# Attention and two expert layers on one core: expert sums in three half-token banks, five banks for attention, and a new order

## The chip, the cores and the metric

The kernel runs on one core of a Trainium2 chip. The metric is the device time of one execution in microseconds (us); lower is better. The core has a matrix engine (PE, TensorE), a vector engine (DVE, VectorE), an activation engine (ACT, ScalarE), a general engine (POOL, GpSimd) and a queue engine for transfers (SP, SyncE). PE adds up its results in eight banks (PSUM) of 512 fp32 columns for each of 128 partitions; DVE and ACT read them there.

## The reference, cut to what matters

```
q_p, k_p = phi(q * 64**-0.25), phi(k * 64**-0.25)      # phi: exp(x @ omega.T - max over the 128 features)
kv, z = sum_s k_p v, sum_s k_p
x = (q_p kv) / (q_p z)                  # 4 batches x 8 heads x 576 tokens x 64 -> 2304 x 512
for layer in (moe, moe2):               # 8 experts, 512 -> 1024 -> 512, one expert for each token
    e = argmax(x @ w_gate);  y = gate * relu(x @ w1[e]) @ w2[e]     # moe: also a sigmoid gate
    x = y
```

The inputs are such that nearly all tokens of a batch choose the same expert. The kernel computes that expert for the whole batch of 576 tokens and mends the tokens that chose another one in a small block at the end.

## The kernel before, in words

Attention works on 16 pairs of heads, four for each batch of 576 tokens (`FORMS` and `TILED` give the form of each). A pair goes through the steps `load_q`, `load_kv`, `q_split`, `q_proj`, `q_exp`, `q_cut`, `k_proj`, `kv`, `num`, `den_a` to `den_c` and `norm`. `k_proj` asks for four PSUM banks at once (`features`, with two calls of `heads`), and all of its matmuls stand ahead of the reads that free these banks. `q_proj` comes in two kinds: where `TILED` is "1" for the batch, one call serves both heads with K = 64 matmuls in fp32 and takes four banks at once; otherwise `q_split` cuts q into a high and a low part first and each head has a call of its own with four fp32r matmuls into two banks. In form "S" `num` is three fp32r products with 288 columns for each half of the tokens, after `q_exp` has made a rounded copy (`qh`) and `q_cut` the rest (`ql`); in form "F" it is one fp32 product, and `q_cut` and the copy fall away.

There are eight expert units, one for each layer and batch, in the order of `ORDERS[3]`. In a unit, `up` makes eight groups (`fc`) of 24 matmuls of 288 columns each, and `down` makes four groups (`c`) of 48. Three matmuls stand for one exact product (high by high, high by low, low by high). A group is one tile `pm` of two banks, one for each half of the tokens, and the halves alternate in the innermost loop. After a group of `up`, ACT writes the relu (`hh`) and DVE the rest (`hl`), each 576 columns wide; after a group of `down`, DVE multiplies by the gate weights (`y`). There are two such tiles, four banks together (`psm`), and the other four (`psa`) serve attention, the gates and the small block. Only the last group of the last unit is done half by half.

The instruction stream is written by one program that gives PE the expert matmuls and calls `slot()` in between; a slot may start up to two attention steps, chosen by a key (`WEIGHTS`, `TWEAKS`) among those that an estimate of the engines' clocks (`Estimate`) calls ready. `Engine` calls go to their queue in the order of the program, and each engine works its queue in order. Before the first unit only attention runs, with seven banks of `psa`; `fill()` gives PE idle matmuls on zeros when nothing is ready. `gate` makes the routing of a batch in several stages, and one bank tile of it (`pg`, `pt`, `pc` or `ptc`) stays in use between two stages. `COPIES` and `START_COPIES` say which engine makes which copy: 0 ACT, 1 DVE, 2 ACT or DVE by an argument (nothing given: ACT).

Of the kernel before, what the change touches and what calls it, by code (L numbers as in the profile page):

```python
# [11 lines left out]
F32 = mybir.dt.float32  # L12
F32R = mybir.dt.float32r
# [11 lines left out]
HS = S // 2  # L25
# [16 lines left out]
TILED = "1100"  # L42
# [11 lines left out]
FORMS = "FRRRFFFSSSSSSSSS"  # L54
CW = 132
XW = 4

WEIGHTS = (-99.0, -99.0, 262.75, -267.46, 198.55, 332.25, -310.29, -471.44, -33.14, 239.82, -489.57, 351.55, -254.05, 173.97)
RAW_WEIGHTS = (-99.0, -99.0, -374.05, -379.93, 519.94, 42.51, 947.74, -153.49, 153.44, 733.35, -182.45, -952.4, -419.2, -198.78)
# [4 lines left out]
PACE = (0.097, 0.001, 1.054, 1.126, 886.024, 3.696, 0.265, 0.264, 1.069, 256.941, 0)  # L64

COPIES = (1, 1, 2, 1, 0, 0, 2)

START_PACE = (0.142, 0.015, 7.433)
START_COPIES = (1, 2, 0, 1, 0, 0, 0)
TWEAKS = {  # L70
    ("den_a", 1): 44.7, ("den_a", 2): 595.6, ("den_a", 3): -18.8, ("den_a", 4): 323.2, ("den_a", 5): 525.4,
    ("den_a", 6): 291.8, ("den_a", 7): -101.8, ("den_a", 8): -71.9, ("den_a", 9): 56.6, ("den_b", 0): 325.6,
    ("den_b", 1): 1.1, ("den_b", 4): 37.9, ("den_b", 5): -9.0, ("den_b", 6): 171.8, ("den_b", 7): 121.2,
    ("den_b", 8): -64.0, ("den_b", 9): -127.0, ("den_c", 0): 75.6, ("den_c", 1): -98.6, ("den_c", 2): 478.0,
    ("den_c", 4): 37.6, ("den_c", 5): -237.6, ("den_c", 6): -550.8, ("den_c", 9): 0.0, ("den_w", 0): 345.4,
    ("den_w", 1): 143.8, ("den_w", 2): 574.5, ("den_w", 3): -16.2, ("den_w", 4): -57.6, ("den_w", 5): -71.8,
    ("den_w", 6): 77.2, ("den_w", 7): 20.5, ("den_w", 8): 24.7, ("den_w", 9): 7.5, ("k_proj", 0): 107.5,
    ("k_proj", 1): -20.1, ("k_proj", 2): 135.6, ("k_proj", 3): -98.0, ("k_proj", 4): -29.4,
    ("k_proj", 5): -51.0, ("k_proj", 6): -49.7, ("k_proj", 8): 473.1, ("k_proj", 9): -623.2, ("kv", 0): -176.7,
    ("kv", 1): -125.4, ("kv", 3): 483.1, ("kv", 4): -62.8, ("kv", 7): -51.7, ("kv", 8): -203.5,  # L80
    ("kv", 9): 650.0, ("norm", 0): 643.8, ("norm", 1): 542.2, ("norm", 2): 77.4, ("norm", 3): -45.2,
    ("norm", 4): -186.2, ("norm", 5): -106.9, ("norm", 6): 227.5, ("norm", 7): 48.0, ("norm", 8): -0.4,
    ("norm", 9): -5.1, ("num", 0): 0.5, ("num", 1): -19.9, ("num", 10): 26.1, ("num", 14): 416.8,
    ("num", 16): 22.8, ("num", 17): 45.6, ("num", 18): 55.1, ("num", 2): -74.7, ("num", 3): 19.4,
    ("num", 4): -844.8, ("num", 6): 170.0, ("num", 7): -558.5, ("q_cut", 1): -198.8, ("q_cut", 11): -85.3,
    ("q_cut", 12): 60.3, ("q_cut", 13): -72.2, ("q_cut", 14): -1186.5, ("q_cut", 16): -207.1,
    ("q_cut", 17): 478.9, ("q_cut", 19): -174.8, ("q_cut", 2): 25.9, ("q_cut", 3): -306.2, ("q_cut", 4): -287.7,
    ("q_cut", 5): -24.0, ("q_cut", 6): -93.1, ("q_cut", 7): -533.3, ("q_cut", 9): -21.1, ("q_exp", 0): -237.5,
    ("q_exp", 1): 916.5, ("q_exp", 10): -245.4, ("q_exp", 11): -365.4, ("q_exp", 13): -179.8,
    ("q_exp", 14): 179.6, ("q_exp", 15): -1328.8, ("q_exp", 17): 117.8, ("q_exp", 18): 181.2,  # L90
    ("q_exp", 19): -23.4, ("q_exp", 2): 343.6, ("q_exp", 3): -348.5, ("q_exp", 5): -38.0, ("q_exp", 6): -20.7,
    ("q_exp", 7): 4.5, ("q_exp", 9): 820.0, ("q_proj", 0): -488.4, ("q_proj", 1): 984.4, ("q_proj", 10): -817.3,
    ("q_proj", 11): -497.2, ("q_proj", 12): 68.1, ("q_proj", 13): -219.8, ("q_proj", 14): -554.4,
    ("q_proj", 16): -308.5, ("q_proj", 19): 96.0, ("q_proj", 3): -28.6, ("q_proj", 4): -32.0,
    ("q_proj", 5): 11.6, ("q_proj", 6): -43.9, ("q_split", 11): -396.2, ("q_split", 14): -317.9,
    ("q_split", 15): 29.6, ("q_split", 17): -159.4, ("q_split", 18): 101.6, ("q_split", 19): -14.0,
    ("q_split", 5): 27.3, ("q_split", 6): -34.7, ("q_split", 7): -89.0, ("q_split", 9): -848.8,
# [3 lines left out]
class Estimate:  # L101
# [24 lines left out]
    def clock(self, begin):  # L126
        while begin >= (self.window + 1) * 3.413:
            if self.slow:
                self.slow = self.work < 0.77 * 3.413
            else:  # L130
                self.slow = self.work < 0.4 * 3.413
            self.window += 1
            self.work = 0.0
        return 2 if self.slow else 1

    def run(self, engine, op, out, ins):
# [8 lines left out]
        elif engine == "tensor":  # L145
# [11 lines left out]
            if rows != self.rows:  # L157
                begin += 0.1
                cost += 0.107
                self.rows = rows  # L160
            cost *= self.clock(begin)
            self.work += cost
# [85 lines left out]
def attention_moe_moe_kernel(ctx, tc, qT, qT2, kT, vp, omst, wg1, wg2, w1a, w2a, w1b, w2b, tabs, eye, outT):  # L248
# [587 lines left out]
    class Unit:  # L836
# [57 lines left out]
        def up(self, x, need, slot):  # L894
            self.h = []
            for fc in range(NFC):
                need(self, fc // 2)
                w = self.w[fc // 2]
                pm = pl.psm.tile([128, 2, 512], F32, tag="pm", name="pm")
                for c in range(NDC):  # L900
                    for i, (wi, xi) in enumerate(((0, 0), (0, 1), (1, 0))):
                        for s in range(2):
                            nc.tensor.matmul(
                                pm[:, s, :HS],
                                w[wi][:, c, fc % 2],
                                x[xi][:, c, tokens(s)],
                                start=c == 0 and i == 0,
                                stop=c == NDC - 1 and i == 2,
                            )
                    if c < NDC - 1:  # L910
                        slot()
                hh = pl.mp.tile([128, 2, HS], F32R, tag="hh", name="hh", bufs=8)
                hl = pl.mp.tile([128, 2, HS], F32R, tag="hl", name="hl", bufs=8)
# [5 lines left out]
                slot()  # L919

        def down(self, need, slot, put, halves=None):
            for c in range(NDC):
                need(self, 4 + c)
                w = self.w[4 + c]
                if halves is not None and c == NDC - 1:
                    pm = pl.psm.tile([128, 2, 512], F32, tag="pm", name="pm")
                    for s in range(2):
                        y = pl.mp.tile([128, S], F32, tag="y", name="y", bufs=4)
                        for fc in range(NFC):
                            for i, (wi, hi) in enumerate(((0, 0), (0, 1), (1, 0))):  # L930
                                nc.tensor.matmul(
                                    pm[:, s, :HS],
                                    w[wi][:, fc, :],
                                    self.h[fc][hi][:, s, :],
                                    start=fc == 0 and i == 0,
                                    stop=fc == NFC - 1 and i == 2,
                                )
                            if fc == 3 or fc == NFC - 1 and s == 0:
                                slot()
                        t = tokens(s)  # L940
                        nc.vector.tensor_tensor(out=y[:, t], in0=pm[:, s, :HS], in1=self.cb[:, t], op=ALU.mult)
                        halves(c, y, s)
                    return
                pm = pl.psm.tile([128, 2, 512], F32, tag="pm", name="pm")
                for fc in range(NFC):
                    for i, (wi, hi) in enumerate(((0, 0), (0, 1), (1, 0))):
                        for s in range(2):
                            nc.tensor.matmul(
                                pm[:, s, :HS],
# [5 lines left out]
                    if fc < NFC - 1:  # L955
                        slot()
                y = pl.mp.tile([128, S], F32, tag="y", name="y", bufs=4)
                nc.vector.tensor_tensor(
                    out=y.rearrange("p (s t) -> p s t", s=2),
                    in0=pm[:, :, :HS],  # L960
                    in1=self.cb.rearrange("p (s t) -> p s t", s=2),
                    op=ALU.mult,
                )
                put(c, y)
                slot()
# [252 lines left out]
    with tc.manual_schedule():  # L1218
# [128 lines left out]
        def run_unit(n, opens=None, block=None):  # L1347
# [11 lines left out]
            if n == 0:  # L1359
                pl.psi = None  # L1360
                psums.close()
                pl.psm = pool(ctx, "psm", 2, space=PSUM)
                pl.psa = pool(ctx, "psa", 4, space=PSUM)
# [15 lines left out]
            else:  # L1379
# [5 lines left out]
                def put(c, y):  # L1385
                    if block is not None:
                        nc.vector.scalar_tensor_tensor(
# [102 lines left out]
```

## Time and profile before

| | before |
|---|---|
| median of 3 runs | 588.97 us (588.17 to 589.77) |
| the profiled execution's own time | 588.86 us |
| its span, first to last instruction | 587.1 us |
| PE busy | 567.9 us, 97% |
| DVE busy | 371.1 us, 63% |
| ACT busy | 225.3 us, 38% |
| POOL busy | 68.4 us, 12% |
| mean granted clock of PE | 0.994 |

The span is the time from the first to the last instruction; 1.8 us of the execution lie around it. Matmuls are pipelined, so their rows overlap: time per matmul is read from start to start. "Idle before" in a row is time in which the engine did nothing before that row, and the name behind the arrow is what ended it.

### The profile page before, as it was taken

The page shows a single profiled execution, that of the slowest core. Times are in us where ns is not written, and L with a number is a line of the kernel's source. Part 1 is how long each engine was busy: PE and PEld are TensorE (multiplying, and loading weights), DVE is VectorE, ACT ScalarE, POOL GpSimd, SP SyncE. Part 2 cuts the span into 40 slices and gives each one's busy share as a digit, 9 for nine tenths or more (in the row PEclk, how much of TensorE's full clock was granted, in tenths as well). Part 3 has the DMA queues.
Part 4 walks back from the last instruction along what each step waited for, and adds up shares of the span by engine and source line. Part 5 has one row for each costly group of instructions (what it writes and reads, how often), then busy time and mean ns, then how long its engine had stood idle before and what let it go on. Part 6 is the DMA issues. An engine that isn't in the chain of part 4 may idle for free.

```text
span 587.1 us, 11426 instructions
## 1 busy us (share of the span) xinstructions
PE 567.9 (97%) x4519; PEld 540.7 (92%) x4519; DVE 371.1 (63%) x695; ACT 225.3 (38%) x503; POOL 68.4 (12%) x48
## 2 busy tenths in 40 slices
PE   8999989999999999999999999999999999999995
PEld 7887779988999999899999999999999999879995
DVE  4487678887775787487866876764545485313522
ACT  6776645224536224424353344322331232324300
POOL 3670500202001130011201210000000000000000
PEclk9999999989999999999999999999999999999998
DMA  9314376525473263283534634544243238664411
GB/s 315 105 62 129 93 231 194 155 87 171 127 171 123 80 217 89 66 272 130 177 94 124 199 103 114 137 150 136 81 118 133 93 95 250 235 218 154 122 41 45
DMA packets 96955, 82.76 MB, mean 141 GB/s; under 512 B 24576, under 2 KB 78464, under 8 KB 96896
## 3 DMA queue, kind: packets, MB, share of 16 engines
q1 hardware_dynamic: 95776, 81.78, 45.1%
q8 instruction: 37, 0.61, 0.4%
q10 hardware_dynamic: 1120, 0.19, 0.2%
q14 instruction: 22, 0.18, 0.1%
HBM read 66.36 MB, written 15.54 MB: 140 GB/s over the span
## 4 chain that ended last, share of the span: by engine, by line
PE 80%; DVE 8%; DMA 5%; issue 3%; ACT 2%; POOL 0%; SPq 0%; ACTq 0%; DVEq 0%; POOLq 0%
PE pm L208 62%; PE pkv L208 5%; PE ph L208 4%; PE pa L208 4%; DMA wr<-w1a 2%; DVE qhh L208 1%; PE pg L208 1%; DMA wr<-w2a 1%; DVE wl L208 1%; DMA qr<-qT 1%; DVE nm L208 1%; ACT wh L208 1%; PE pby L208 1%; DMA rdd<-dt 1%; ACT kp L208 1%
## 5 line engine op out<-in xcount | busy, mean ns | idle before, releaser
L208 PE MATMUL pm<-xh,wh 128*128 128x288 f32 x512 | 113.4, 303 | 1.6 <-DVE hl L208 1.3
L208 PE MATMUL pm<-hh,wh 128*128 128x288 f32 x512 | 114.2, 302 | 0.6 <-DVE y L208 0.6
L208 PE MATMUL pm<-hh,wl 128*128 128x288 f32 x512 | 111.4, 297 | 0.0
L208 PE MATMUL pm<-hl,wh 128*128 128x288 f32 x512 | 111.3, 297 | 0.0
L208 PE MATMUL pm<-xh,wl 128*128 128x288 f32 x512 | 109.6, 296 | 0.5 <-DVE wl L208 0.5
L208 PE MATMUL pm<-xl,wh 128*128 128x288 f32 x512 | 109.5, 295 | 0.0
L208 POOL PARTITION_ALL_REDUCE qhl<-qhh x32 | 67.2, 2139 | 282.8 <-DVE qhh L208 185.2
L208 ACT CAST wh<-wr 128x1024 fp32r<-128x1024 f32 (+1 forms) x72 | 67.8, 951 | 55.5 <-PE pm L208 40.5
L208 PEld LDWEIGHTS pm<-xh,wh 128*128 128x128 f32 x512 | 82.1, 189 | 5.7 <-DVE hl L208 2.3
L208 PEld LDWEIGHTS pm<-hh,wh 128*128 128x128 f32 x512 | 82.9, 190 | 4.4 <-issue 3.0
L208 DVE TENSOR_TENSOR wl<-wr,wh 128x1024 fp32r<-128x1024 f32 (+1 forms) x72 | 78.5, 1103 | 12.6 <-ACT wh L208 12.2
L208 PEld LDWEIGHTS pm<-hh,wl 128*128 128x128 f32 x512 | 83.3, 190 | 0.0
L208 PEld LDWEIGHTS pm<-hl,wh 128*128 128x128 f32 x512 | 83.2, 190 | 0.0
L208 DVE SCALAR_TENSOR_TENSOR hl<-pm,hh 128x576 fp32r<-128x576 f32 x64 | 48.4, 757 | 54.8 <-ACT hh L208 53.9
L208 PEld LDWEIGHTS pm<-xh,wl 128*128 128x128 f32 x512 | 82.4, 188 | 0.7 <-DVE wl L208 0.7
L208 PEld LDWEIGHTS pm<-xl,wh 128*128 128x128 f32 x512 | 82.3, 188 | 0.0
L208 ACT ACTIVATE hh<-pm 128x576 fp32r<-128x576 f32 x64 | 41.7, 651 | 73.3 <-PE pm L208 73.2
L208 DVE TENSOR_TENSOR y<-pm,cb 128x576 f32<-128x576 f32 (+1 forms) x33 | 24.3, 737 | 58.4 <-PE pm L208 58.3
L208 ACT ACTIVATE kp<-ph,nm 128x128 f32<-128x128 f32 x140 | 38.0, 387 | 21.1 <-DVE nm L208 19.2
L208 ACT ACTIVATE qhh<-qhh 128x576 f32<-128x576 f32 x32 | 22.1, 706 | 58.3 <-DVE qhh L208 56.1
L208 DVE TENSOR_REDUCE nm<-ph 128x3 f32<-128x384 f32 (+1 forms) x64 | 27.2, 484 | 14.2 <-PE ph L208 14.1
L208 PEld LDWEIGHTS pkv<-vt,kp 128*128 128x128 f32 x280 | 32.6, 192 | 1.5 <-ACT ev L208 0.8
(145 smaller groups left out, 580.0 us busy)
## 6 DMA issues: line engine op xcount, KB each, us to landing
wr<-w2a SPq DMA_DIRECT2D x16, 512.0 KB, 4.1
wr<-w2b SPq DMA_DIRECT2D x16, 512.0 KB, 3.9
qr<-qT SPq DMA_DIRECT2D x24, 288.0 KB, 4.3
wr<-w1a SPq DMA_DIRECT2D x12, 512.0 KB, 4.7
wr<-w1b SPq DMA_DIRECT2D x12, 512.0 KB, 3.9
vt<-vp SPq DMA_DIRECT2D x16, 325.0 KB, 4.5
kr<-kT SPq DMA_DIRECT2D x16, 288.0 KB, 4.4
xd<-xraw SPq DMA_DIRECT2D x16, 288.0 KB, 3.5
```

Source lines behind the costliest of these rows:

```text
L208: return f(*args, **kw)
```

## The change

`up` and `down` take the two halves of the tokens one after the other, each in a tile `pm` of one bank; `hh`, `hl` and `y` become two instructions of 288 columns each. Three such banks are in turn (`PMB`), and `psa` gets five. In the last unit every group is written out half by half, where before only its last one was. The slots stand as often as before, one for every six matmuls.

`TILED` and `FORMS` move work of batch 2: its four pairs use the tiled `q_proj` (no `q_split`), and its first and third pair have form "F". The keys that order the attention steps, the paces and the places of copies are new: after the start the copies `qh` and all copies of `q_proj` are on ACT, in the start the weights' rounded copies and half of the copies of `num` are on DVE. The estimate's clock model is changed as well (it has no instruction of its own on the chip, but it chooses the order).

```diff
-TILED = "1100"
+TILED = "1110"
-FORMS = "FRRRFFFSSSSSSSSS"
+FORMS = "FRRRFFFSFSFSSSSS"
+PMB = 3
-WEIGHTS = (-99.0, -99.0, 262.75, -267.46, ...
+WEIGHTS = (-99.0, -99.0, 422.84, -661.91, ...
-PACE = (0.097, 0.001, 1.054, 1.126, 886.024, 3.696, 0.265, 0.264, 1.069, 256.941, 0)
+PACE = (0.068, 0.001, 0.116, 0.951, 1127.16, 262.576, 0.142, 0.249, 0.287, 240.646, 0)
-COPIES = (1, 1, 2, 1, 0, 0, 2)
+COPIES = (1, 2, 0, 1, 0, 0, 0)
-START_PACE = (0.142, 0.015, 7.433)
-START_COPIES = (1, 2, 0, 1, 0, 0, 0)
+START_PACE = (0.014, 0.009, 30.436)
+START_COPIES = (2, 1, 2, 1, 1, 2, 0)
 TWEAKS = {
...
+            busy = cost
+            if op != "transpose" and ins[-1].dtype == F32:
+                busy = 4 * n / 2400 * cost / (2 * max(2 * n / 2400 + 0.002, 0.111) + (0.107 if turn else 0))
...
-                pm = pl.psm.tile([128, 2, 512], F32, tag="pm", name="pm")
-                for c in range(NDC):
-                    for i, (wi, xi) in enumerate(((0, 0), (0, 1), (1, 0))):
-                        for s in range(2):
+                for s in range(2):
+                    pm = pl.psm.tile([128, 512], F32, tag="pm", name="pm")[:, :HS]
+                    for c in range(NDC):
+                        for i, (wi, xi) in enumerate(((0, 0), (0, 1), (1, 0))):
...
-                    if c < NDC - 1:
-                        slot()
-                nc.scalar.activation(hh, pm[:, :, :HS], AF.Relu)
-                nc.vector.scalar_tensor_tensor(
-                    out=hl, in0=pm[:, :, :HS], scalar=0.0, in1=hh.bitcast(F32), op0=ALU.max, op1=ALU.subtract
-                )
+                        if c == 1:
+                            slot()
+                    nc.scalar.activation(hh[:, s], pm, AF.Relu)
+                    nc.vector.scalar_tensor_tensor(
+                        out=hl[:, s], in0=pm, scalar=0.0, in1=hh[:, s].bitcast(F32), op0=ALU.max, op1=ALU.subtract
+                    )
+                    slot()
...
-        def down(self, need, slot, put, halves=None):
+        def down(self, need, slot, put, half=None):
...
-                pm = pl.psm.tile([128, 2, 512], F32, tag="pm", name="pm")
-                for fc in range(NFC):
-                    for i, (wi, hi) in enumerate(((0, 0), (0, 1), (1, 0))):
-                        for s in range(2):
+                y = pl.mp.tile([128, S], F32, tag="y", name="y", bufs=4)
+                for s in range(2):
+                    pm = pl.psm.tile([128, 512], F32, tag="pm", name="pm")[:, :HS]
+                    for fc in range(NFC):
+                        for i, (wi, hi) in enumerate(((0, 0), (0, 1), (1, 0))):
...
+                        if fc % 2 and fc < NFC - 1:
+                            slot()
+                    nc.vector.tensor_tensor(out=y[:, tokens(s)], in0=pm, in1=self.cb[:, tokens(s)], op=ALU.mult)
+                    if half is not None:
+                        half(c, y, s)
+                    elif s:
+                        put(c, y)
+                    slot()
...
-                pl.psm = pool(ctx, "psm", 2, space=PSUM)
-                pl.psa = pool(ctx, "psa", 4, space=PSUM)
+                pl.psm = pool(ctx, "psm", PMB, space=PSUM)
+                pl.psa = pool(ctx, "psa", 8 - PMB, space=PSUM)
```

## Rows read from the trace of the kernel before

**Rows 1.** The page's first part: busy time, share of the span, instructions.
```profile
PE 567.9 (97%) x4519; PEld 540.7 (92%) x4519; DVE 371.1 (63%) x695; ACT 225.3 (38%) x503; POOL 68.4 (12%) x48
```

**Rows 2.** Stages: busy time and count by engine, granted clock, DMA share, GB/s.
```profile
0.00:71.90 71.90, 68.24 (x574) 56.69 (x574) 45.74 (x104) 49.82 (x156) 33.76 (x32) 1.00 0.42 137
...
123.10:129.50 6.40, 5.06 (x35) 4.74 (x35) 4.95 (x12) 2.94 (x11) 0.00 (x0) 0.75 0.26 74
129.50:376.00 246.50, 243.24 (x1968) 238.26 (x1967) 180.30 (x328) 101.54 (x220) 29.92 (x14) 1.00 0.47 141
376.00:581.00 205.00, 203.06 (x1582) 194.97 (x1581) 96.87 (x187) 52.20 (x85) 0.00 (x0) 1.00 0.44 136
```

**Rows 3.** The chain of waits that ended last: start, duration, what.
```profile
533.80 43.17 PE pm L208 x324
```

**Rows 4.** Timeline of PE: k_proj cut in two, and one whole.
```profile
123.10 1.16 PE L208 MATMUL ph<-om,kr 64*128 64x128 f32 x14
125.60 0.71 PE L208 MATMUL ph<-om,kr 64*128 64x128 f32 x6 [1.34 <-ACT kp L208]
126.24 0.84 PE L208 MATMUL pm<-hh,wh 128*128 128x288 f32 x2
...
174.23 1.70 PE L208 MATMUL ph<-om,kr 64*128 64x128 f32 x20
175.87 0.40 PE L208 MATMUL pm<-xh,wh 128*128 128x288 f32 x1
...
236.19 0.71 PE L208 MATMUL ph<-om,kr 64*128 64x128 f32 x6 [1.35 <-ACT kp L208]
```

**Rows 5.** Timeline of all engines, the gate's tile pt: written, and last read.
```profile
122.80 0.38 PE L208 MATMUL pt<-ident,lg 128*72 128x128 f32 x2
...
127.62 0.26 ACT L208 COPY ls<-pt 72x128 f32<-72x128 f32 x1
```

**Rows 6.** Timeline of PE before the first unit: tiled q_proj, num in form F.
```profile
31.19 1.24 PE L208 MATMUL ph<-qr,om 64*128 64x288 f32 x8
32.37 1.89 PE L208 MATMUL pkv<-vt,kp 128*128 128x65 f32 x15
...
53.76 1.24 PE L208 MATMUL pa<-qhh,kvr 128*128 128x288 f32 x4
54.83 0.80 PE L208 MATMUL pf<-ident,xt 128*128 128x128 f32 x5
55.78 1.78 PE L208 MATMUL ph<-qr,om 64*128 64x288 f32 x8
57.49 2.50 PE L208 MATMUL pkv<-vt,kp 128*128 128x128 f32 x20
```

**Rows 7.** Timeline of all engines, a late release of expert banks in the first unit.
```profile
82.05 0.63 ACT L208 ACTIVATE hh<-pm 128x576 fp32r<-128x576 f32 x1
...
83.53 0.53 PE L208 MATMUL pm<-xh,wh 128*128 128x288 f32 x2 [1.30 <-DVE hl L208]
```

**Rows 8.** Timeline of PE at the end, the two halves of the last group.
```profile
576.67 0.29 PE L208 MATMUL pm<-hh,wl 128*128 128x288 f32 x1
577.51 0.40 PE L208 MATMUL pm<-hh,wh 128*128 128x288 f32 x1 [0.55 <-DVE y L208]
...
580.68 0.29 PE L208 MATMUL pm<-hh,wl 128*128 128x288 f32 x1
```

**Rows 9.** Groups by shape: count, busy us, mean ns, idle before.
```profile
L208 DVE SCALAR_TENSOR_TENSOR hl<-pm,hh 128x576 fp32r<-128x576 f32 x64 | 48.4, 757 | 54.8 <-ACT hh L208 53.9
L208 ACT ACTIVATE hh<-pm 128x576 fp32r<-128x576 f32 x64 | 41.7, 651 | 73.3 <-PE pm L208 73.2
L208 DVE TENSOR_TENSOR qs<-qr,qs 64x576 fp32r<-64x576 f32 x16 | 14.6, 911 | 0.6
L208 ACT COPY ev<-pa 128x288 f32<-128x288 f32 x26 | 10.0, 411 | 7.6 <-PE pa L208 3.4 <-PE pm L208 2.1 <-DVE xraw L208 1.9
L208 PE MATMUL idle<-zeros 128*128 128x256 bf16 x54 | 7.8, 300 | 1.1 <-POOL zeros L208 1.1
L208 DVE TENSOR_TENSOR y<-pm,cb 128x288 f32<-128x288 f32 x2 | 0.9, 458 | 4.5 <-PE pm L208 4.5
```

More of the change, by code (lines that the diff above doesn't have):

```diff
@@ L70 @@
-TWEAKS = {
[L71 to L97, printed above, removed]
@@ new lines @@
+PMB = 3
+WEIGHTS = (-99.0, -99.0, 422.84, -661.91, 253.95, 357.57, -428.34, -229.86, -148.38, 428.38, -402.99, 446.43, -85.76, 85.92)
+RAW_WEIGHTS = (-99.0, -99.0, -376.15, -302.92, 64.37, -269.47, 1065.34, -141.53, 154.83, 521.33, 294.97, -1106.64, -315.4, -68.93)
+PACE = (0.068, 0.001, 0.116, 0.951, 1127.16, 262.576, 0.142, 0.249, 0.287, 240.646, 0)
+COPIES = (1, 2, 0, 1, 0, 0, 0)
+START_PACE = (0.014, 0.009, 30.436)
+START_COPIES = (2, 1, 2, 1, 1, 2, 0)
+TWEAKS = {
+    ("den_a", 0): -90.8, ("den_a", 1): 23.5, ("den_a", 2): 595.6, ("den_a", 3): 45.5, ("den_a", 4): -152.5,
+    ("den_a", 5): 893.0, ("den_a", 6): 56.9, ("den_a", 7): -336.0, ("den_a", 8): 33.9, ("den_a", 9): 20.0,
+    ("den_b", 0): 128.1, ("den_b", 1): 165.0, ("den_b", 2): -9.7, ("den_b", 3): 21.4, ("den_b", 4): -78.3,
+    ("den_b", 5): 73.2, ("den_b", 6): 155.4, ("den_b", 7): -2.1, ("den_b", 8): 225.3, ("den_b", 9): 611.8,
+    ("den_c", 0): 1090.2, ("den_c", 1): -191.8, ("den_c", 2): 139.8, ("den_c", 4): 3.8, ("den_c", 6): -158.9,
+    ("den_c", 7): 35.8, ("den_c", 8): -100.7, ("den_c", 9): -10.2, ("den_w", 0): 127.9, ("den_w", 1): -27.9,
+    ("den_w", 2): 66.9, ("den_w", 3): -403.8, ("den_w", 4): -322.5, ("den_w", 5): -195.3, ("den_w", 6): -103.7,
+    ("den_w", 7): -330.4, ("den_w", 9): 515.1, ("k_proj", 0): 15.6, ("k_proj", 1): 127.2, ("k_proj", 2): -43.1,
+    ("k_proj", 3): 243.8, ("k_proj", 4): 595.5, ("k_proj", 5): 18.2, ("k_proj", 6): 39.3, ("k_proj", 7): -35.3,
+    ("kv", 0): -283.2, ("kv", 1): 1.2, ("kv", 2): -27.3, ("kv", 3): 44.8, ("kv", 4): -7.5, ("kv", 5): 171.1,
+    ("kv", 6): 318.5, ("kv", 7): -783.4, ("kv", 8): 106.5, ("kv", 9): 433.3, ("norm", 0): 84.6,
+    ("norm", 2): -26.9, ("norm", 3): -35.9, ("norm", 4): -20.2, ("norm", 5): -133.2, ("norm", 6): -33.3,
+    ("norm", 7): -662.5, ("norm", 8): 106.2, ("norm", 9): -135.4, ("num", 0): 79.3, ("num", 1): 37.6,
+    ("num", 10): 45.1, ("num", 11): 77.0, ("num", 17): 1547.6, ("num", 19): -42.6, ("num", 2): 10.3,
+    ("num", 3): 4.8, ("num", 5): 40.3, ("num", 6): 25.0, ("num", 7): 127.1, ("num", 8): 124.3,
+    ("num", 9): 209.0, ("q_cut", 10): -1210.4, ("q_cut", 11): -327.9, ("q_cut", 12): -222.8,
+    ("q_cut", 14): 19.9, ("q_cut", 15): -12.5, ("q_cut", 16): 94.9, ("q_cut", 17): 1.6, ("q_cut", 2): -40.0,
+    ("q_cut", 4): -390.5, ("q_cut", 5): -36.2, ("q_cut", 6): -46.5, ("q_cut", 7): -1360.6, ("q_cut", 8): 199.6,
+    ("q_cut", 9): 684.6, ("q_exp", 0): 95.4, ("q_exp", 1): 1833.0, ("q_exp", 10): 189.6, ("q_exp", 12): 12.1,
+    ("q_exp", 14): 1.2, ("q_exp", 15): -893.3, ("q_exp", 18): -40.1, ("q_exp", 19): -46.8, ("q_exp", 3): 189.2,
+    ("q_exp", 4): 221.7, ("q_exp", 5): -1072.2, ("q_exp", 8): 607.2, ("q_exp", 9): -62.0, ("q_proj", 0): 855.6,
+    ("q_proj", 1): 1968.8, ("q_proj", 11): 152.8, ("q_proj", 14): 597.4, ("q_proj", 15): 102.3,
+    ("q_proj", 16): 238.2, ("q_proj", 17): -87.6, ("q_proj", 18): -99.2, ("q_proj", 2): -286.5,
+    ("q_proj", 4): 53.5, ("q_proj", 6): 7.0, ("q_proj", 8): -186.0, ("q_split", 1): 184.3,
+    ("q_split", 10): 382.5, ("q_split", 13): -0.5, ("q_split", 14): 6.2, ("q_split", 15): -39.1,
+    ("q_split", 16): -1.5, ("q_split", 18): -11.1, ("q_split", 3): 426.3, ("q_split", 4): 23.1,
+    ("q_split", 5): 13.1, ("q_split", 6): -0.8, ("q_split", 7): 15.5, ("q_split", 9): 547.9,
@@ L130, in clock @@
             else:
-                self.slow = self.work < 0.4 * 3.413
+                self.slow = self.work < 0.5 * 3.413
             self.window += 1
@@ L156, in run @@
             rows = 64 if ins[-1].shape[0] == 64 else 32 if out.shape[0] == 32 else 128
-            if rows != self.rows:
+            turn = rows != self.rows
+            if turn:
                 begin += 0.1
@@ L160, in run @@
                 self.rows = rows
-            cost *= self.clock(begin)
-            self.work += cost
+            busy = cost
+            if op != "transpose" and ins[-1].dtype == F32:
+                busy = 4 * n / 2400 * cost / (2 * max(2 * n / 2400 + 0.002, 0.111) + (0.107 if turn else 0))
+            clock = self.clock(begin)
+            cost *= clock
+            self.work += busy * clock
             end = self.now[engine] = begin + cost
@@ L898, in up @@
                 w = self.w[fc // 2]
-                pm = pl.psm.tile([128, 2, 512], F32, tag="pm", name="pm")
-                for c in range(NDC):
-                    for i, (wi, xi) in enumerate(((0, 0), (0, 1), (1, 0))):
-                        for s in range(2):
+                hh = pl.mp.tile([128, 2, HS], F32R, tag="hh", name="hh", bufs=8)
+                hl = pl.mp.tile([128, 2, HS], F32R, tag="hl", name="hl", bufs=8)
+                for s in range(2):
+                    pm = pl.psm.tile([128, 512], F32, tag="pm", name="pm")[:, :HS]
+                    for c in range(NDC):
+                        for i, (wi, xi) in enumerate(((0, 0), (0, 1), (1, 0))):
                             nc.tensor.matmul(
-                                pm[:, s, :HS],
+                                pm,
                                 w[wi][:, c, fc % 2],
@@ L924, in down @@
                 w = self.w[4 + c]
-                if halves is not None and c == NDC - 1:
-                    pm = pl.psm.tile([128, 2, 512], F32, tag="pm", name="pm")
-                    for s in range(2):
-                        y = pl.mp.tile([128, S], F32, tag="y", name="y", bufs=4)
-                        for fc in range(NFC):
-                            for i, (wi, hi) in enumerate(((0, 0), (0, 1), (1, 0))):
[L931 to L947, printed above, removed]
+                y = pl.mp.tile([128, S], F32, tag="y", name="y", bufs=4)
[3 more added lines that the diff above has]
+                        for i, (wi, hi) in enumerate(((0, 0), (0, 1), (1, 0))):
                             nc.tensor.matmul(
-                                pm[:, s, :HS],
+                                pm,
                                 w[wi][:, fc, :],
@@ L954, in down @@
                             )
[L955 to L965, printed above, removed]
+                        if fc % 2 and fc < NFC - 1:
+                            slot()
+                    if half is not None and s:
+                        y = pl.mp.tile([128, S], F32, tag="y", name="y", bufs=4)
+                    nc.vector.tensor_tensor(out=y[:, tokens(s)], in0=pm, in1=self.cb[:, tokens(s)], op=ALU.mult)
[4 more added lines that the diff above has]
+                    slot()
     def left(l):
@@ L1385, in put @@
                 def put(c, y):
-                    if block is not None:
-                        nc.vector.scalar_tensor_tensor(
-                            out=y, in0=block.y[c], scalar=state[:, 8], in1=y, op0=ALU.mult, op1=ALU.add
-                        )
                     dst = outT[c * 128 : (c + 1) * 128, u.b * S : (u.b + 1) * S]
```

5 lines of the change are left out of this document (removed).

## The prediction

> **What bounds the kernel now.** I read the page's busy times first: PE has work for 97% of the span [rows 1], and no other engine comes near. The stages say where the rest is [rows 2]. In the last long stage, 376 to 581, where only experts and the small block are left, PE is busy 203.06 of 205.00 us; from 129.5 to 376, with attention woven in, 243.24 of 246.50. Both run at the full granted clock, 1.00, which is the level of 2.4 GHz. So PE's own stream sets the end, and a change can only win by taking matmuls out, by closing the holes between them, or at the two ends.
>
> The price of an expert matmul comes from the chain of waits, whose longest piece is 324 of them in 43.17 us [rows 3]: 133 ns each. There are 3072 (six groups of 512), 409 us, and the change leaves their number and width alone. Does the other loop order alter their pitch? The last group of the kernel before has already the new form, 24 matmuls on one half of the tokens in one bank, then 24 on the other. From 577.51 to 580.68 lie 23 steps in 3.17 us, 138 ns with the first, slower step behind a wait in them [rows 8]. I take the pitch as unchanged.
>
> **The holes.** The timeline of PE has one form of hole that the bank count explains. A `k_proj` is 20 matmul records. Whole, it takes from 174.23 to 175.87, 1.64 us; at 123.10 it stands still after 14 records and goes on at 125.60, when ACT has read the first of its own banks, and the next expert matmul begins at 126.24 [rows 4]. That is 3.14 us, so the hole costs 1.50. The reason is beside it: the gate's tile `pt`, written at 122.80, is last read at 127.62 [rows 5]. It holds one of the four banks of `psa`, and `k_proj` wants four. There are two more holes of this form, each with a bank tile of the gate in use; the last waits 1.35 us [rows 4]. I price the three at 1.50 each: 4.5 us. Behind the first hole the granted clock falls: 0.75 over the 6.40 us from 123.10 [rows 2], that is the level of 1.2 GHz for about half of them, which costs a quarter of 6.40, 1.6 us.
>
> The second form of hole is a late release of expert banks: 1.30 us at 83.53 for `hl`, since ACT began the `hh` of an earlier group only at 82.05, behind other work in its queue [rows 7]. The third is at the very end: from 576.67 to 577.51 are 0.84 us where 0.13 are due, as the second half of the last group waits for DVE's reading of the first half of the same tile [rows 8].
>
> **The change part by part.**
>
> *Five banks for attention.* Four heads and one gate tile fit together, so the three holes close: -4.5 us. But the change adds four more requests for four banks at once (the tiled `q_proj` of batch 2) to the eight `k_proj` that run beside experts, and two bank tiles alive at the time would stall any of these twelve. Before, three of eight met a held bank; that share of twelve would be 4.5 stalls, 6.8 us, the upper bound; none is the lower. One bank more makes it rarer, so I take one of 1.5 us: +1.5. The clock's fall came behind such a hole; I take back three quarters of its 1.6: -1.2 (bounds: all of it, or one fall more, +1.6).
>
> *Expert banks by halves.* Two tiles of two banks gave a release the time of the other tile's group, 24 x 0.133 = 3.2 us; three banks give it two groups of 12, again 3.2 us. What must be done in that time shrinks: before, `hh` 0.651 and `hl` 0.757, 1.41 us [rows 9]; after, by the nearest rows of 288 columns read from a bank, ACT's 0.411 and DVE's 0.458, 0.87 us. So 0.54 us more slack in the same queues. I take half of the 1.30: -0.65. Neither `hh` nor `hl` is on the path elsewhere: in the stage from 129.5 ACT is busy 101.5 of 246.5 us and DVE 180.3 [rows 2]. More instructions cost these engines time: 128 x 0.411 against 41.7 us is 11 us more on ACT, 128 x 0.458 against 48.4 is 10 us more on DVE. The cover is PE's work; without it the price is the delay of a release beyond 3.2 us.
>
> *The end.* Each half has a tile of its own in the last group too, so the wait for `y` goes: -0.7. Behind the last matmul stands the same half-wide `y`, its addition and the last transfer, so the tail stays.
>
> *Forms of batch 2.* Two pairs lose three fp32r products in `num`: 6 x 0.133 = 0.80 us for a head, against 1.07 for the fp32 form (53.76 to 54.83) [rows 6]: +0.27, four heads, +1.1. The tiled `q_proj` is 1.18 us at its quickest (31.19 to 32.37) and 1.71 at 55.78 [rows 6], against 8 x 0.133 = 1.07 for two untiled calls: +0.1 to +0.65 for each of four pairs. I take +0.25, nearer to the quick one, as banks make the difference: +1.0 (bounds +0.4, +2.6). What falls away is DVE's: eight subtractions of 0.911 us [rows 9], 7.3 us, with their casts, and the cutting of two pairs. The copies moved to ACT, 14 `qh` of 576 columns and eight of 288 for batch 3, are 36 times 288 columns at 0.411 [rows 9], 15 us; with the 11 us for `hh` ACT gets some 26 us heavier, and DVE by the same copies and the subtractions lighter. Both are hidden behind PE, and I count nothing; uncovered, it shows as a release that comes late in ACT's queue (below). The loads of q for batch 2 halve; no PE wait in this trace is put down to q's transfer, so nothing again.
>
> *Another order, other copies in the start.* Until 71.9 PE is busy 68.24 us [rows 2], but 54 of the records there are idle matmuls, 7.8 us [rows 9], a part of them before the first data. A better order can win at most those and the 3.7 us not busy; a worse one can lose as much. I count nothing. Nor do I for the holes not named so far, among them most of the 1.94 us from 376 on [rows 2]: others like them will come in their place.
>
> Sum, against the profiled execution's 588.86 us: -4.5 +1.5 -1.2 -0.65 -0.7 +1.1 +1.0 = -3.45, which gives **585.4 us**. That execution lies 0.1 us below the median of the runs, 588.97, so the sum needs no shift. About 0.3%, 1.8 us, is what a measurement of this kernel can tell from no change.
>
> **The rivals.**
>
> *1. The holes only move.* Four-bank requests go from eight to twelve; if the new order puts the tiled `q_proj` next to a `num` or a `k_proj` whose banks are still held, 4.5 stalls come in place of three. Then the terms are -4.5 +6.8 -0.65 -0.7 +1.1 +1.0 = +3.0 at worst, and with three stalls and no win of clock 589.1: no change. For it: the order is chosen by readiness of data and estimated engine clocks, and `pt` was held across a `k_proj` already. Against it: one held bank was enough before, two are needed now.
>
> *2. Slower: ACT's queue releases the expert banks late.* All copies of `q_proj`, the `qh` copies and twice as many `hh` stand in ACT's queue, in order, and an `exp` that waits for DVE or POOL holds up the `hh` behind it. At 83.53 this cost 1.30 us once [rows 7]. There are 80 half groups of `up` in the five units that run beside attention. From 5.25 / 1.3 = four such waits on, the gain is gone and the loss can be measured; eight give 585.4 + 10.4 = 595.8. Against it: ACT is under half busy in that stage, and the work per release falls by 0.54 us.
>
> *3. Slower: the clock.* The one fall beside experts cost 1.6 us [rows 2], and it came behind a hole of 1.34 us [rows 4]. If banks changed twice as often leave PE short pauses that bring five falls, the time is 585.4 + 8 = 593.4. Against it: the last 24 matmuls before the wait and the 24 after it, in single banks, show no fall, and neither does the long stage at 1.00. The Trainium skill, page "TensorE: Matmul & The Clock Gate", section "A second HAM failure mode: psum-queue depth-cycling", describes just this: cycling through PSUM banks leaves small pauses between groups, and the clock goes back and forth. This trace doesn't show it for the old grouping.
>
> *4. Much faster: the start too.* If the new order also removes most of the idle matmuls and of the other holes, some 5 us more go: 580.
>
> **How the numbers follow.** Forecast (about 582 to 587) 0.45; the holes move, 587.2 to 591: 0.20; ACT's queue 0.15; clock 0.06; the start too, under 582: 0.14. Under the forecast's lower half and the fourth rival lie nearly all cases that are faster by over 0.3% (below 587.2): 0.58. Within 0.3% (to 590.7): 0.19. Slower: 0.23. The range leaves out the far ends, a tenth on either side: from the fourth rival with a little more, 579, to the half-way cases of the second and third, 592.5. Most of the chance has two signs, so the forecast's own range, by the bounds of its terms: -4.5 -1.6 -1.3 -0.7 +1.1 +0.4 = -6.6 to -4.5 +3.0 -0.7 +1.1 +2.6 = +1.5, so 582.3 to 590.4.
>
> **What would show it.** Right: whole `k_proj` of 20 records beside a held gate tile, with no wait for `kp`; 24 and 24 matmuls at the end without the 0.7 us; the stage from 376 on as long as before but for that; a clock near 1.00 in every stage up to the last matmul. Wrong: waits of `ph` for ACT's copies `qhh` (rival 1); waits of `pm` for `hl` or `hh` in several places (rival 2); stages with a granted clock of 0.9 or less (rival 3); a first unit that begins well before or after 71.9 (rival 4, or its opposite).

## The result and the profile after

The changed kernel takes 583.66 us (median of 6 runs, 581.53 to 583.70) against 588.57 us beside it (6 runs, 587.17 to 589.84): a ratio of 0.991, 95% interval 0.989 to 0.993. That is 4.9 us faster; 585.4 was forecast, with -3.45 us as the sum. The profiled execution took 583.70 us, its span is 581.9 us. The page's first part, to stand beside [rows 1]:

```profile
PE 563.2 (97%) x4509; PEld 534.8 (92%) x4509; DVE 357.0 (61%) x745; ACT 244.9 (42%) x589; POOL 69.6 (12%) x48
```

PE has 4.7 us less busy time, though its rows differ by ten records only. DVE is 14 us lighter, ACT 20 us heavier. By stages, to stand beside [rows 2] (columns as there):

```profile
0.00:72.80 72.80, 67.84 (x591) 56.66 (x592) 50.92 (x119) 49.66 (x158) 34.35 (x32) 1.00 0.49 160
72.80:370.00 297.20, 293.07 (x2371) 283.51 (x2372) 207.51 (x418) 140.03 (x326) 35.23 (x16) 1.00 0.47 142
370.00:576.00 206.00, 202.33 (x1549) 194.62 (x1547) 97.82 (x208) 55.16 (x105) 0.00 (x0) 0.99 0.43 133
```

The first unit begins 0.9 us later (72.81 against 71.87), with one `k_proj` more already done. From there to the last matmul it is 502.9 us, before 509.1. The gain lies where experts and attention run together: from the first matmul of the first expert unit to the first of the seventh it is 377.4 us, before 386.1, while the last two units take 2.4 us more than before, a part of it lost clock. Who PE waits for (us in total, times, longest):

```profile
PE pm L215 <- DVE hl L215: 3.5, 3, 1.6
PE pst L215 <- issue: 2.5, 1, 2.5
...
PE ph L215 <- ACT kp L215: 0.2, 1, 0.2
```

The cut `k_proj` of [rows 4] is gone: the only wait of `ph` for `kp` left is 0.2 us, ahead of the first unit. Beside experts a `k_proj` now looks like this in the timeline of PE, 1.31 us from its start to that of the next expert matmul:

```profile
113.44 1.39 PE L215 MATMUL ph<-om,kr 64*128 64x128 f32 x20
114.75 0.40 PE L215 MATMUL pm<-hh,wh 128*128 128x288 f32 x1
```

But waits of `pm` for `hl` went from one of 1.30 us [rows 7] to three, 3.5 us together. Each has something else ahead of the read in its queue. For the wait at 80.91 it is DVE's queue: `hh` was done by 77.4, but `hl` came behind the steps that finish a piece of attention's output, `xl` the last of them. For the one at 85.63 it is ACT's: `hh` came behind an exponential that waited for DVE and a copy `qh` that the change has moved to ACT. The third, 0.87 us at 473.85, stands in DVE's queue behind small steps that prepare the small block.

```profile
79.73 0.76 DVE L215 TENSOR_TENSOR xl<-xraw,xh 128x576 fp32r<-128x576 f32 x1
80.40 0.45 DVE L215 SCALAR_TENSOR_TENSOR hl<-pm,hh 128x288 fp32r<-128x288 f32 x1
80.91 0.40 PE L215 MATMUL pm<-xh,wh 128*128 128x288 f32 x1 [1.60 <-DVE hl L215]
...
83.38 0.69 ACT L215 ACTIVATE qhh<-qhh 128x576 f32<-128x576 f32 x1 [1.91 <-DVE qhh L215]
84.10 0.67 ACT L215 CAST qh<-qhh 128x576 fp32r<-128x576 f32 x1
84.68 0.40 ACT L215 ACTIVATE hh<-pm 128x288 fp32r<-128x288 f32 x1
```

And the wait ahead of the small block's transposes (`pst`), 1.24 us before, is 2.51 us. The timeline of PE in the kernel before, then of PE and of DVE in the changed one, shows what it is:

```profile
496.70 0.61 PE L208 MATMUL pst<-ident,sel 128*96 128x128 f32 x4 [1.24 <-issue]
```

```profile
486.55 0.29 PE L215 MATMUL pm<-hh,wl 128*128 128x288 f32 x1
489.35 1.06 PE L215 MATMUL pst<-ident,sel 128*96 128x128 f32 x4 [2.51 <-issue]
```

```profile
484.39 1.36 DVE L215 TENSOR_TENSOR_SCAN pos<-ones,sel 128x576 f32<-128x576 f32 x1
488.07 0.46 DVE L215 TENSOR_TENSOR y<-pm,cb 128x288 f32<-128x288 f32 x1 [2.31 <-DMA cb<-cohd]
488.44 0.81 DVE L215 SCALAR_TENSOR_TENSOR sel<-pos,state,sel 128x576 f32<-128x576 f32 x1
```

The first `y` of a unit is due after 24 matmuls of `down` now and no longer after 48. Here it came before its gate weights (`cb`) had landed, DVE stood still for 2.31 us, and `sel`, queued behind that `y`, was late for PE. The clock fell behind this hole:

```profile
486.00:500.00 14.00, 11.49 (x81) 11.17 (x80) 7.05 (x12) 3.04 (x7) 0.00 (x0) 0.88 0.65 215
```

At the end the two halves run through. To stand beside [rows 8], the timeline of PE across the last two groups:

```profile
572.23 0.29 PE L215 MATMUL pm<-hh,wl 128*128 128x288 f32 x1
572.36 0.30 PE L215 MATMUL pm<-hh,wh 128*128 128x288 f32 x1
...
575.43 0.29 PE L215 MATMUL pm<-hh,wl 128*128 128x288 f32 x1
```

From 572.36 there are 24 matmuls up to 575.43, and the step into them is 0.13 us where it was 0.84. The groups by shape, to stand beside [rows 9]:

```profile
L215 DVE SCALAR_TENSOR_TENSOR hl<-pm,hh 128x288 fp32r<-128x288 f32 x128 | 57.1, 454 | 63.9 <-ACT hh L215 63.3
L215 ACT ACTIVATE hh<-pm 128x288 fp32r<-128x288 f32 x128 | 51.9, 414 | 81.7 <-PE pm L215 81.3
L215 DVE TENSOR_TENSOR y<-pm,cb 128x288 f32<-128x288 f32 x64 | 29.1, 455 | 76.5 <-PE pm L215 74.1 <-DMA cb<-cohd 2.3
L215 PE MATMUL idle<-zeros 128*128 128x256 bf16 x52 | 7.6, 302 | 1.1 <-POOL zeros L215 1.1
```

The half-wide reads cost 0.414 and 0.454 us, as estimated (0.411 and 0.458).

### The profile page after: what moved, and what is told of

Same layout as the page of the kernel before. It is cut to its first block, busy times and chain, and to the rows that moved or that the text cites. A ratio compares the mean times of both kernels' runs of the same rounds, so it can differ in the third digit from the quotient of the medians.

```text
span 581.9 us, 11530 instructions
## 1 busy us (share of the span) xinstructions
PE 563.2 (97%) x4509; PEld 534.8 (92%) x4509; DVE 357.0 (61%) x745; ACT 244.9 (42%) x589; POOL 69.6 (12%) x48
## 4 chain that ended last, share of the span: by engine, by line
PE 82%; DVE 6%; DMA 4%; issue 3%; ACT 3%; SPq 0%; POOL 0%; DVEq 0%; POOLq 0%; ACTq 0%
PE pm L215 64%; PE pkv L215 5%; PE ph L215 4%; PE pa L215 4%; DMA wr<-w1a 4%; PE pg L215 1%; ACT qhh L215 1%; DVE qhh L215 1%; ACT wh L215 1%; DVE wl L215 1%; DVE xh L215 1%; PE pby L215 1%; DVE nm L215 1%; DMA om<-omst 1%; PE pxt L215 0%
## 5 line engine op out<-in xcount | busy, mean ns | idle before, releaser
L215 PE MATMUL pm<-xh,wh 128*128 128x288 f32 x512 | 154.7, 302 | 5.1 <-DVE hl L215 3.5
L215 PE MATMUL pm<-hh,wh 128*128 128x288 f32 x512 | 155.0, 303 | 0.0
L215 PE MATMUL pm<-hl,wh 128*128 128x288 f32 x512 | 151.3, 296 | 0.0
L215 PE MATMUL pm<-hh,wl 128*128 128x288 f32 x512 | 151.3, 296 | 0.0
L215 PE MATMUL pm<-xh,wl 128*128 128x288 f32 x512 | 151.1, 295 | 0.1
L215 PE MATMUL pm<-xl,wh 128*128 128x288 f32 x512 | 150.9, 295 | 0.0
L215 DVE SCALAR_TENSOR_TENSOR hl<-pm,hh 128x288 fp32r<-128x288 f32 x128 | 57.1, 454 | 63.9 <-ACT hh L215 63.3
L215 ACT ACTIVATE hh<-pm 128x288 fp32r<-128x288 f32 x128 | 51.9, 414 | 81.7 <-PE pm L215 81.3
L215 DVE TENSOR_TENSOR y<-pm,cb 128x288 f32<-128x288 f32 x64 | 29.1, 455 | 76.5 <-PE pm L215 74.1
L215 PE MATMUL pkv<-vt,kp 128*128 128x128 f32 (+1 forms) x280 | 33.8, 276 | 0.0
```

The source lines that it names most:

```text
L215: return f(*args, **kw)
```

## The experiments

Each ratio is to the kernel before, measured beside the run, with its 95% interval. The kernel before took 588.1 to 589.8 us beside these runs, so a difference between two experiments is told to about 1 us. Where an experiment changes the banks "in the same order", the estimate that chooses the order still reckons with three and five, so that every engine's instructions are those of the unaltered kernel, one for one.

**1. The fifth attention bank away, same order.**

```diff
-pl.psa = pool(ctx, "psa", 8 - PMB, space=PSUM)
+pl.psa = pool(ctx, "psa", 4, space=PSUM)
+pl.psa.bufs = 5          # what the estimate reckons with
```

> The changed kernel, instruction for instruction in the same order, with four banks for attention in place of five (one bank of the core lies unused). Theory A, the fifth bank closes the holes: twelve four-bank requests stand beside experts, and those that meet a held bank wait again for ACT, at some 1.5 us each; with three to six of them and a fall of the granted clock 588 to 594 us. Theory B, the new order and not the bank made the gain: the requests stand where banks are free anyway, 583 to 585 us and no k_proj cut in two.

583.29 us, ratio 0.990 (0.988 to 0.992): as fast as the changed kernel. No `k_proj` is cut. One tiled `q_proj` takes longer, 131.00 to 132.92, against 1.17 us from 130.37 in the changed kernel:

```profile
131.00 1.99 PE L215 MATMUL ph<-qr,om 64*128 64x288 f32 x8
132.92 0.40 PE L215 MATMUL pm<-hh,wh 128*128 128x288 f32 x1
```

The cause is the one that theory A names: the gate's tile `pg`, whose matmuls run from 129.88, is read only at 133.32.

```profile
133.32 0.29 ACT L215 COPY lg<-pg 128x144 f32<-128x144 f32 x1
```

In the changed kernel `pg` is in use across the same `q_proj` (until 132.52), but there the fifth bank is free. So of the 11 four-bank requests beside experts one meets a held bank, and it costs 0.75 us, not 1.5; experiments 7, 8 and 12, with four banks too, show the same step at 1.9 us. For the time as a whole theory B holds for this order: it puts its `k_proj` where four banks are free.

**2. The old keys on the new bank plan.** `WEIGHTS`, `RAW_WEIGHTS`, `PACE`, `COPIES`, `START_PACE`, `START_COPIES` and `TWEAKS` are those of before; everything else is the changed kernel.

```diff
-TWEAKS = {("den_a", 0): -90.8, ("den_a", 1): 23.5, ...
+TWEAKS = {("den_a", 1): 44.7, ("den_a", 2): 595.6, ...
...
-COPIES = (1, 2, 0, 1, 0, 0, 0)
+COPIES = (1, 1, 2, 1, 0, 0, 2)
```

> The changed kernel with the keys, paces and places of copies of the kernel before; half banks, five banks for attention and the forms of batch 2 stay. Theory A (banks): no k_proj is cut in two, at most one hole of that form, 584 to 587.5 us. Theory B (order): the gain is gone, 588 to 592 us.

588.50 us, ratio 0.999 (0.997 to 1.000): no gain, as theory B has it. Yet no `k_proj` is cut here either, as theory A has it; the holes are of the other form. PE's waits:

```profile
PE pm L215 <- DVE hl L215: 7.2, 5, 2.8
PE ph L215 <- DMA kr<-kT: 1.3, 1, 1.3
PE ptc L215 <- DVE g L215: 1.3, 1, 1.3
```

One of the five, 1.61 us at 300.75, shows its cause in ACT's timeline: ACT stands still 5.29 us until DVE has an exponential's input ready, and three `hh`, on each of which the release of an expert bank hangs, stand behind it. The longest, 2.83 us at 86.60, begins in ACT's queue too, with a cast that waits 2.77 us for a transfer of weights. The other three don't show ACT's queue alone: at 161.72 (0.85 us) casts of weights stand ahead in both queues, and at 242.75 and 484.14 (0.99 and 0.87 us) `hh` was done and `hl` stood in DVE's queue behind small steps of a gate and of the small block.

```profile
297.45 0.69 ACT L215 ACTIVATE qhh<-qhh 128x576 f32<-128x576 f32 x1 [5.29 <-DVE qhh L215]
298.04 1.03 ACT L215 CAST wh<-wr 128x1024 fp32r<-128x1024 f32 x1
298.98 1.00 ACT L215 ACTIVATE hh<-pm 128x288 fp32r<-128x288 f32 x3
```

**3. The new keys on the old bank plan.** The kernel before, with the keys, forms and estimate of the changed one, but its loops, two expert tiles of two banks and four banks for attention.

```diff
-TILED = "1100"
+TILED = "1110"
...
 pl.psm = pool(ctx, "psm", 2, space=PSUM)      # as before
 pl.psa = pool(ctx, "psa", 4, space=PSUM)
```

> The kernel before with the new keys, paces, places of copies, forms and estimate, but its expert tiles of two banks, two of them, and four banks for attention. Theory A (banks): holes of 1.5 us at four-bank requests as before or more of them, 587 to 593 us. Theory B (order): the gain is there without the banks, 583 to 586 us.

588.72 us, ratio 1.000 (0.998 to 1.002): no gain. PE waits once 4.4 us for `hl`, in the first unit behind ACT's queue, and once 1.4 us in a cut `k_proj`:

```profile
PE pm L214 <- DVE hl L214: 4.4, 1, 4.4
...
PE ph L214 <- ACT kp L214: 1.6, 2, 1.4
```

The new keys don't make the gain by themselves. This order is the one that the keys give with the old plan; experiment 1, with the same keys and four banks for attention too, but three half banks for the experts, is 5.4 us faster with one bank less in all.

**4. The small block's selection called ready later.**

```diff
+est.written[sel.tensor.name] += 3.0
 yield [sel]
```

> The changed kernel, with the selection of the small block called ready 3 us later in the estimate, so that its transposes stand 24 expert matmuls later. In the changed kernel PE waits 2.5 us before them at 486.6, as DVE's selection stands behind a y that waits for the gate weights' transfer, and the granted clock is 0.88 over the 14 us from there. If that wait is all: 2.5 us less for the hole and up to 1.7 for the clock, 579.5 to 581.5 us. If the wait only moves to the next thing that is late: 583 to 584 us.

579.79 us, ratio 0.985 (0.983 to 0.987), about 4 us under the changed kernel. DVE's `y` still waits for `cb` (2.40 us), but PE has other work in that time. The hole is gone and the clock behind it stays up:

```profile
486.00:500.00 14.00, 13.89 (x110) 13.62 (x110) 8.46 (x14) 3.49 (x7) 0.00 (x0) 1.00 0.67 204
```

So PE's wait there, 1.24 us of it in the kernel before already, cost the changed kernel about four microseconds with the fall of clock behind it. The clock fell once here too, but in the first unit: 0.91 over the 18.00 us from 72.00, where the changed kernel has 1.00. That doesn't touch the four: the changed kernel's wait of 1.60 us for `hl` in that stretch is gone here, and from the unit's first matmul to the end of its next wait for `hl` it is 12.8 us in both.

**5. The old keys with four attention banks**, the order of experiment 2, one for one.

```diff
 # on top of experiment 2
+pl.psa = pool(ctx, "psa", 4, space=PSUM)
+pl.psa.bufs = 5
```

> The second run's kernel (old keys, half banks), in the same order, with four banks for attention in place of five. Theory A (the fifth bank closes the holes where an order puts a four-bank request beside a held tile, and the new keys avoid such places): k_proj is cut in two again at one to three places, 1.5 us each, 590 to 594 us against its 588.5. Theory C (the bank never mattered, under either order): 588 to 589 us, no k_proj cut.

595.38 us, ratio 1.008 (1.005 to 1.012): 6.9 us above experiment 2, 5.7 by the two ratios, and above the 594 that was expected at most. Here `k_proj` is cut again, 14 records and 6, in the very form of [rows 4]:

```profile
128.43 1.16 PE L215 MATMUL ph<-om,kr 64*128 64x128 f32 x14
130.99 0.71 PE L215 MATMUL ph<-om,kr 64*128 64x128 f32 x6 [1.40 <-ACT kp L215]
...
155.73 1.16 PE L215 MATMUL ph<-om,kr 64*128 64x128 f32 x14
158.23 1.22 PE L215 MATMUL ph<-om,kr 64*128 64x128 f32 x6 [1.34 <-ACT kp L215]
```

Theory A holds for this order, C falls: here the fifth bank is what closes these holes. Not all of the difference is the bank's. The first unit of the profiled execution begins 2.2 us later than in experiment 2 (73.30 against 71.06), and until then the two kernels have the same banks; from there to the last matmul it is 4.4 us. The mean granted clock is 0.988 against 0.993, with one fall of it in that start.

**6. Two expert half banks, same order as the changed kernel.**

```diff
-pl.psm = pool(ctx, "psm", PMB, space=PSUM)
+pl.psm = pool(ctx, "psm", 2, space=PSUM)
+pl.psm.bufs = 3
```

> The changed kernel in the same order, with two expert half banks in place of three (one bank unused). A release then has the time of one group of 12 matmuls, 1.6 us, instead of 3.2. hh and hl take 0.41 and 0.45 us and two semaphores, so a release in an empty queue fits. If late releases in the queues of ACT and DVE are what the third bank covers: of 128 groups of up some 20 to 40 are late by 0.3 to 1 us, 592 to 610 us. If the queues are mostly empty when a group ends: 584 to 587 us.

602.76 us, ratio 1.022 (1.020 to 1.024), by the ratios 18 us above the changed kernel:

```profile
PE pm L215 <- DVE hl L215: 16.8, 22, 3.2
PE pm L215 <- DVE y L215: 2.1, 2, 1.7
```

As the first theory had it, 22 releases come later than one group of 1.6 us allows, by 0.76 us on average. In the profiled execution the granted clock is 1.00 from 72.8 to 590 all the same; its mean over the execution is 0.999, and 0.993 to 0.996 in the four others, so some clock was lost there.

**7. Four expert banks and four for attention, same order.**

```diff
+pl.psm = pool(ctx, "psm", 4, space=PSUM)
+pl.psm.bufs = 3
+pl.psa = pool(ctx, "psa", 4, space=PSUM)
+pl.psa.bufs = 5
```

> The changed kernel in the same order, with four expert half banks and four for attention. The first run showed that this order does without the fifth attention bank. A release then has three groups, 4.8 us. The three waits of pm for hl in the changed kernel (1.6, 1.0 and 0.9 us) should fall away or shrink, the wait before the small block's transposes should stay: 580 to 582 us. If the waits for hl were not set by the number of banks: 583 to 584 us.

585.01 us, ratio 0.992 (0.990 to 0.994): no better than the changed kernel, and above both ranges. All waits of `pm` for `hl` are gone, as expected, but others grew:

```profile
PE pst L215 <- issue: 3.8, 1, 3.8
PE ph L215 <- ACT ev L215: 2.5, 1, 2.5
```

A tiled `q_proj` at 84.50, in reach of PE sooner now and with the fifth attention bank missing, stands after half of its records until ACT has read `num`'s banks. And since PE comes to the transposes 1.8 us earlier, their wait grows from 2.5 to 3.8 us: what it waits for hangs on a transfer, and the `y` behind that transfer is only 0.7 us earlier (487.40 against 488.07).

**8. Both repairs together**, the banks of experiment 7 in the order of experiment 4.

```diff
+est.written[sel.tensor.name] += 3.0
...
+pl.psm = pool(ctx, "psm", 4, space=PSUM)
+pl.psa = pool(ctx, "psa", 4, space=PSUM)
```

> Four expert half banks and four for attention, in the order of the fourth run (the selection called ready 3 us later). If both repairs add up: 577 to 578.5 us, against 579.8 of the fourth run. If the hl waits were slack that another wait takes: 579 to 580.5 us.

579.53 us, ratio 0.983 (0.981 to 0.985): they don't add up. PE waits 2.0 us at the transposes again and 1.3 us at that `q_proj`.

**9 and 10. Both kernels without keys for single steps.**

```diff
-TWEAKS = {
...
-}
+TWEAKS = {}
```

> The changed kernel with no key for single steps (the table TWEAKS empty), so that only the general weights order attention. With the next run it compares the two bank plans at an order that is fitted to neither step by step. Theory D (the bank plan is better by itself, whatever the order): clearly below the next run, by 3 us or more. Theory E (the plan pays only with an order fitted to it): within 2 us of the next run or above it, both above 590 us.

> The kernel before with the table TWEAKS empty. Theory D: 3 us or more above the run beside it. Theory E: within 2 us of it or below it; both theories: slower than the kernel before, 592 to 605 us.

594.36 us for the changed kernel, ratio 1.009 (1.005 to 1.012), and 617.34 us for the one before, ratio 1.048 (1.044 to 1.052). The new kernel lies 23 us lower at an order not fitted step by step, as theory D has it; the 617 lie above the 605 expected at most. The two still differ in general weights, paces, forms and places of copies, so the 23 us aren't the banks' alone.

**11. The old places of copies.**

```diff
-COPIES = (1, 2, 0, 1, 0, 0, 0)
+COPIES = (1, 1, 2, 1, 0, 0, 2)
-START_COPIES = (2, 1, 2, 1, 1, 2, 0)
+START_COPIES = (1, 2, 0, 1, 0, 0, 0)
```

> The changed kernel with the places of copies of the kernel before (qh and half of the q_proj copies back on DVE; in the start the weights' copies on ACT), new keys. If the load moved from DVE to ACT is a part of the gain: late releases through DVE, 586 to 590 us. If it is not: 582 to 585 us.

582.15 us, ratio 0.988 (0.984 to 0.991). The load moved from DVE to ACT is no part of the gain that could be measured. The order is not frozen here, since the estimate reckons with the places: PE waits 1.3 us for `hl` in place of 3.5, but 2.8 us for `wh` at the first unit's start in place of 1.6.

**12. Four and four, the gate weights' transfer earlier, the selection later still.**

```diff
-if i == 3:
+if i == 2:
...
-est.written[sel.tensor.name] += 3.0
+est.written[sel.tensor.name] += 7.0
```

> Four expert half banks and four for attention, the gate weights' transfer asked for two weight chunks earlier, one chunk of up ahead of before, and the selection called ready 7 us later. If y's wait for that transfer is what still held the transposes in the eighth run (2.0 us and a slow clock behind them): 576 to 578 us. If another wait takes its place: 578.5 to 580.5 us.

578.75 us, ratio 0.982 (0.979 to 0.985). The wait at the transposes is gone, the one at the `q_proj` is 3.2 us:

```profile
PE ph L215 <- ACT ev L215: 3.2, 1, 3.2
PE pm L215 <- DVE wh L215: 1.6, 1, 1.6
```

Another wait took the place, as the second expectation said. `y` doesn't wait for `cb` any more here; as the selection was called later in the same run, the two edits aren't told apart. The intervals of experiments 4, 8 and 12 overlap; each is some 4 to 5 us faster than the changed kernel, and the one line of experiment 4 is enough for that.

## Why the prediction was right, and where it was not

**The holes at `k_proj`.** The three closed, and they are the largest part of the gain. Two things in this step were off. The size: a whole `k_proj` is 1.31 us, not the 1.64 of the one that I took (in the kernel before, the four other whole ones beside experts take 1.31 to 1.32), and so each hole was worth 3.14 - 1.31 = 1.83 us, 5.5 for three instead of 4.5. The stall that I had added for twelve requests (+1.5; there are 11 beside experts) did not come. And the cause: I put it to the fifth bank. Experiment 1 shows that the new order cuts no `k_proj` even with four banks and meets one held bank, for 0.75 us, at a tiled `q_proj`. Experiment 5 against 2 shows that the bank does what I said where an order needs it. So bank and order are two ways to close the same holes; in the changed kernel the order alone suffices for `k_proj`.

**The order.** "I count nothing" was the weakest step. Keys and bank plan each give nothing alone (experiments 2 and 3, 588.50 and 588.72) and 4.9 us together. With the old keys on the new plan the rival of late releases comes true: five of them, 7.2 us, though only two of the five, 4.4 us, begin in ACT's queue.

**Expert banks by halves.** The term was -0.65, as the work per release shrinks. That work shrank as predicted (0.87 us), but the waits for `hl` rose from 1.30 to 3.5 us, +2.2, so the sign was wrong. What is late is not the two reads but what stands ahead of them in ACT's or DVE's queue, and the 0.54 us of slack did not cover it. That the time allowed matters was right: with one group less PE waits 16.8 us for `hl` (experiment 6), with one more not at all (experiment 7).

**The clock.** I took back 1.2 of 1.6 us. It fell once again, elsewhere: 0.88 over 14.0 us, which is 1.7 us, behind the wait at `pst`. Not foreseen was that a half group's `y` comes due 24 matmuls earlier and meets a transfer; that wait, 2.51 against 1.24, and the fall behind it are what experiment 4 wins back. The traces bear out that the loops bring it: DVE's `y` waits 2.3 to 3.9 us for `cb` there in the changed kernel and in every run with its loops, under either order, but for experiment 12, which asks for the transfer earlier; with the old loops (before, experiments 3 and 10) it doesn't wait. How long PE waits then hangs on the order: 0.81 us in experiment 2, whose transposes stand 12 expert matmuls later. The third rival did not come: from 72.8 to 370 the bank changes every 12 or 24 matmuls at a clock of 1.00, and so it does in the profiled execution of experiment 6, with 22 short waits. The cycling through banks that the Trainium skill describes (page "TensorE: Matmul & The Clock Gate", section "A second HAM failure mode: psum-queue depth-cycling") did not by itself bring the clock down in these two executions.

**The end** gave the 0.7 us. **The forms** cost less than +2.1: the tiled `q_proj` is 1.17 us beside experts, its lower bound, and I see no hole of it in the changed kernel. Summed from start to start beside experts, the four take 4.7 us where the untiled calls took 4.5, and form "F" takes 3.3 us more where the fp32r products of `num` take 2.9 less: +0.5 together.

Worked out from the rows: k_proj 3 x -1.83, `hl` +2.2, `pst` +1.3, clock about 0, end -0.7 make -2.7. Of the other 2.5 us, the later start with one `k_proj` of 1.31 us more in it gives -0.4, and the smaller waits of before in the first unit (for `wl`, `wh` and `xraw`, 0.5 to 0.6 us each) another 1.6, less some 0.5 for the forms; about 1 us is spread over the rest and not traced further.

That the sum came within 1.8 us of the result is partly luck. The end was right and the holes nearly so, but the terms for the stall, the clock, `hl` and the forms were off by 1.5, 1.2, 2.9 and 1.6 us, and nothing was counted for the start, the small waits and `pst`; these errors have both signs and largely cancel. Two figures of the prediction don't follow from its own terms: three stalls without a win of clock give 589.6, not 589.1, and the range's upper end takes +3.0 in all for the stalls and the clock, where the bounds named were +6.8 and +1.6. The result touches neither.

What stays open is how much of the gain a different search of keys would give the old bank plan: the runs show only that the new keys are not it. No run has the old forms of batch 2 or the old clock model of the estimate under the new keys, so what these two are worth for the order is not shown.

## What to carry to other kernels

Where a program picks its instruction order by an estimate, bank plan and order are one change: test each on the other's partner, and freeze the order when you change a resource, or you measure the order. Before you cut a result into smaller pieces, look at what the first piece needs: it comes due earlier, and an in-order engine that waits for it holds up all that is queued behind. A closed hole is worth its own length only up to the next thing that keeps its own time, as a transfer does.

## What the runs showed of the hardware that was not expected

A tile's granularity has a price too: with both halves in one tile, PE waited 0.55 us at the end for DVE's reading of the other bank, and with a tile for each half the step is 0.13 us. In the profiled execution of experiment 6, 22 waits of 0.76 us on average did not bring PE's granted clock down from 2.4 GHz, while single holes of 1.34 us (before) and 2.51 us (after) each had a fall to 1.2 GHz behind them, worth 1.6 and 1.7 us. The length of a hole doesn't decide it: in the kernel before, the cut `k_proj` that waits 1.35 us [rows 4] has a clock of 1.00 about it (230 to 245), and other executions of the same kernel have mean clocks from 0.991 to 0.999. A fall behind one hole of one trace is thus no fixed price of such a hole.
